# A forward list scheduler in place of a gap-filling one, for an eight-request decode kernel

## The chip, the cores and the metric

The kernel runs on one core of a Trainium2 chip. The core has a matrix engine (TensorE, PE), a vector engine (VectorE, DVE), a scalar engine (ScalarE, ACT) and a general one (GpSimd, POOL); a fifth queue (SyncE, SP) issues the DMA transfers. Each engine works off its own instruction stream strictly in the order in which the program was written for it, and waits on semaphores where it needs another engine's result. The metric is the device time of one execution in microseconds; lower is better.

## The reference

Eight requests (batch 8, one token each, width 448) pass through four layers: attention, MLP, and the same attention and MLP again, each behind a layer norm and with a residual. Both attentions use the same cache, of which only the last 1024 positions count.

```python
def _A_ref(x, k_cache, v_cache, wq, wo):         # Hq 16, Hkv 8, Dh 256, W 1024
    q = (x @ wq).reshape(B, Sq, Hq, Dh).transpose(0, 2, 1, 3)
    k = jnp.repeat(k_cache[:, :, Sk - W:, :], rep, axis=1)
    v = jnp.repeat(v_cache[:, :, Sk - W:, :], rep, axis=1)
    scores = jnp.einsum("bhqd,bhkd->bhqk", q, k) * (Dh ** -0.5)
    o = jnp.einsum("bhqk,bhkd->bhqd", _softmax(scores, axis=-1), v)
    return o.transpose(0, 2, 1, 3).reshape(B, Sq, Hq * Dh) @ wo
def _B_ref(x, w1, w2):                           # F 1792
    return jnp.einsum("bsf,fd->bsd", _silu(jnp.einsum("bsd,df->bsf", x, w1)), w2)

x = x + _A_ref(_layernorm(x), A_k_cache, A_v_cache, A_wq, A_wo)
x = x + _B_ref(_layernorm(x), B_w1, B_w2)
x = x + _A_ref(_layernorm(x), A_k_cache, A_v_cache, A_wq, A_wo)
x = x + _B_ref(_layernorm(x), B_w1, B_w2)
```

## The kernel before

**The work of one request.** The kernel goes through the requests b = 0 to 7. The keys and values of one request are 16 loads of 512 KB, into a ring of 29 buffers (`slots`). Below, number 0 behind a letter is the first attention, 1 the second.

1. `KT` (L879): DVE transposes the eight key buffers in place, two instructions per buffer, 16 per request.
2. `S0` (L600): 64 score matmuls of the first attention, in two halves `S0.0` and `S0.1` of four heads each. The query blocks `qbd` for them come from POOL (`qbd1`, L568), two instructions per request. Then the softmax: maximum (L606), three small DVE steps `mT`, `mg`, `mb` (L612 to L616), two exponentials on ACT (L620), a transposition on PE (`pT`, L625) and its copy (L629).
3. `PV0` (L657 in row form, L686 in column form), then `wo` (L728), a fold that adds the partial rows (L752, L497), and the new x (`xbt`, L699).
4. The chain of the MLP: statistics (L703, L705), mean and variance on DVE (L708 to L713), the power on POOL (L715), `w1` (L490), tanh (L768), `w2` (L773), a fold, the new x (`x2b`, L699), statistics again.
5. `wq` (L786): the queries of the second attention, two halves of 16 matmuls, each copied by ACT (`qrow`, L791), turned by PE (L794), and made into the blocks of `qbd` (L579, L583), with the factor `maskr` (L781).
6. `S1` (two halves again, L600), its softmax, and `PV1` (L657). The last two layers behind it are done for all eight requests together at the end (L809 to L847).

`keep` (L745) are matmuls with zeros into columns that nothing reads.

**What ties requests together.** All work of POOL stands in program order, since every POOL task writes the key `pool_serial`; so `qbd1` of request b+1 comes behind the second power of request b. `mT` is one tile for both attentions, so the softmax of `S0` of request b+1 comes behind that of `S1` of request b. `S1.0` frees four key slots, and into them go the last three value loads of request b+1; the second half of `S1` and `PV1` free the rest.

**What sets the order.** No order is written by hand. Every piece of work is a `Task` with an engine, a duration (`dur`) and the keys that it reads and writes; `Plan.add` derives the dependences from the keys. `Plan.schedule` (L78 to L165) then gives every task a rank (the longest way from it to the end, by the durations and the latencies `LAT`), takes the ready tasks by rank, and puts each into the first gap of its engine that is long enough and not before its inputs are ready. A task taken later can so land ahead of one taken earlier. Loads keep their program order; a DVE task that reads a load counts the load as landed 1.5 us later (`LOAD_MARGIN`). The times of this plan only sort the tasks: `Plan.emit` writes each engine's stream in the order of the planned starts, with the semaphore waits that this order needs.

Of the kernel before, what the change touches and what calls it, by code (L numbers as in the profile page):

```python
# [1 line left out]

# [8 lines left out]
ACTF = mybir.ActivationFunctionType  # L11
AX = mybir.AxisListType

SEM_LAT = {"pe": 0.05, "dve": 0.04, "act": 0.04, "pool": 0.06, "sp": 0.06}
LAT = {"pe": 0.15, "dve": 0.07, "act": 0.09, "pool": 0.05, "sp": 0.0}
LOAD_MARGIN = 1.5


class Task:
    __slots__ = ("eng", "fns", "dur", "prio", "name", "deps", "idx", "ready", "end", "sem", "val",  # L20
                 "vc", "n_bytes", "start", "users", "rank")

    def __init__(self, eng, fns, dur, prio, name, n_bytes=0):
        self.eng, self.fns, self.dur, self.prio, self.name = eng, fns, dur, prio, name
        self.n_bytes = n_bytes
        self.deps = {}
        self.users = 0
        self.end = None


class Plan:
# [43 lines left out]
        self.tasks.append(t)  # L75
        return t

    def schedule(self, dma_lat=2.1):  # L78


        tasks = self.tasks
        n_left = [len(t.deps) for t in tasks]
        succ = [[] for _ in tasks]
        for t in tasks:
            for i in t.deps:
                succ[i].append(t)
        sp_next = [t for t in tasks if t.eng == "sp"]
        nxt = {}
        for a, b in zip(sp_next, sp_next[1:]):
            nxt[a.idx] = b  # L90
        for t in reversed(sorted(tasks, key=lambda t: t.idx)):
            r = 0.0
            for u in succ[t.idx]:
                lat = (0.0 if t.eng == "pe" else 0.04) if t.eng == u.eng else LAT[t.eng] + 0.05
                r = max(r, u.rank + lat)
            if t.eng == "sp":
                own = t.dur
                t.rank = max(own + dma_lat + r, (own + nxt[t.idx].rank) if t.idx in nxt else 0.0)
            else:
                t.rank = t.dur + r  # L100
        gaps = {e: [[0.0, 1e9]] for e in ("pe", "dve", "act", "pool")}
        sp_pos, sp_free, dma_free = 0, 0.0, 0.0
        heap, seq = [], 0

        def push(t):
            heapq.heappush(heap, ((-t.rank if t.eng != "sp" else -1e9), t.idx, t))

        def ready_of(t):
            r = 0.0
            for o, raw in t.deps.values():  # L110
                if o.eng != t.eng or o.eng == "sp":
                    lat = LOAD_MARGIN if o.eng == "sp" and t.eng == "dve" else LAT[o.eng]
                    r = max(r, o.end + lat + SEM_LAT[t.eng])
                elif raw and t.eng in ("dve", "act"):
                    r = max(r, o.end + LAT[t.eng] + 0.04)
                else:
                    r = max(r, o.end)
            return r

        for t in tasks:  # L120
            if n_left[t.idx] == 0 and t.eng != "sp":
                push(t)
        if n_left[sp_next[0].idx] == 0:
            push(sp_next[0])
        done = 0
        while heap:
            _, _, t = heapq.heappop(heap)
            r = ready_of(t)
            if t.eng == "sp":
                t.start = max(r, sp_free)  # L130
                sp_free = t.start + 0.6
                s = max(t.start + 0.3, dma_free)
                dma_free = s + t.dur
                t.end = dma_free + dma_lat
                sp_pos += 1
                if sp_pos < len(sp_next) and n_left[sp_next[sp_pos].idx] == 0:
                    push(sp_next[sp_pos])
            else:
                g = gaps[t.eng]
                for k, (g0, g1) in enumerate(g):  # L140
                    s = max(g0, r)
                    if s + t.dur <= g1 + 1e-9:
                        break
                t.start, t.end = s, s + t.dur
                new = []
                if s - g0 > 0.02:
                    new.append([g0, s])
                if g1 - t.end > 0.02:
                    new.append([t.end, g1])
                g[k:k + 1] = new  # L150
            done += 1
            for u in succ[t.idx]:
                n_left[u.idx] -= 1
                if n_left[u.idx] == 0:
                    if u.eng != "sp":
                        push(u)
                    elif sp_pos < len(sp_next) and u is sp_next[sp_pos]:
                        push(u)
        assert done == len(tasks), "no task can run"
        self.order = {e: sorted((t for t in tasks if t.eng == e), key=lambda t: (t.start, t.end))  # L160
                      for e in ("pe", "dve", "act", "pool")}
        self.order["sp"] = sp_next
        self.span = max(t.end for t in tasks)
        self.busy = {e: sum(t.dur for t in self.order[e]) for e in self.order}
        return self.order  # L165

    def emit(self):
# [85 lines left out]
def bass_interleave_layers__sliding_block_cached__dense_activation_silu__decode_kernel(  # L253
    nc, A_x, A_k_cache, A_v_cache, A_wq, A_wo, B_x, B_w1, B_w2, out
):
    NB, Sq, D = A_x.shape
    _, HKV, SK, DH = A_k_cache.shape
    HD = A_wq.shape[1]
    H = HD // DH
    F = B_w1.shape[1]  # L260
    W = min(4096, max(256, SK // 4))
    S0 = SK - W
    P = 128
# [45 lines left out]
    vn = sb("vn", [P, 1], F32)  # L309
# [42 lines left out]
    def bk(i):  # L352
        return [("bank", i)]
# [4 lines left out]
    def dve(fn, reads, writes, dur, prio, name=""):  # L358
        add("dve", fn, reads=reads, writes=writes, dur=max(0.06, dur - LAT["dve"]), prio=prio, name=name)
# [68 lines left out]

    def load_wo():
        dma(lambda e: e.dma_start(wo_sb[:].rearrange("p (c n) -> p c n", n=D),  # L430
                                  A_wo.rearrange("(c p) n -> p c n", p=P)), ["wo"], HD * D * 2, "wo", rate=340e3)

    def load_w2():
        dma(lambda e: e.dma_start(w2_sb[:].rearrange("p (c n) -> p c n", n=D),
                                  B_w2.rearrange("(c p) n -> p c n", p=P)), ["w2"], F * D * 2, "w2", rate=340e3)

    WO_R = ["wo"]
    W2_R = ["w2"]
# [10 lines left out]
    def load_v(s, b, g):  # L449
        if g >= 4:  # L450
            dma(lambda e: e.dma_start(slots[s][:, :].rearrange("v (q n) -> v q n", q=4),
                                      A_v_cache[b, g, S0:SK, :].rearrange("(q v uh) d -> v q (uh d)", q=4, uh=2)),
                [("slot", s)], W * DH * 2, "slot%d" % s, rate=340e3)
# [3 lines left out]
        dma(lambda e: e.dma_start(slots[s][:, :].rearrange("v (j n) -> v j n", j=4),  # L457
                                  src.rearrange("j (v uh) d -> v j (uh d)", uh=2)),
            [("slot", s)], W * DH * 2, "slot%d" % s, rate=340e3)


    def wq_l(o, i):
# [146 lines left out]

    def softmax(b, layer, prio):  # L610
        sc, lb, ei = SC[layer], LB[layer], layer
        dve(lambda e: e.transpose(mT[ei][:], mseg[ei][:]), [("mseg", ei), ("mseg", ei, 0), ("mseg", ei, 1)], ["mT"], 0.21, prio)  # L612
        dve(lambda e: e.tensor_reduce(
            mg[ei][:], mT[ei][:, 0:8].rearrange("p (q r) -> p r q", r=2), AX.X, ALU.min),
            ["mT"], [("mg", ei)], 0.16, prio)
        dve(lambda e: e.transpose(mb[ei][:].rearrange("p (q r) -> p q r", r=2),  # L616
                                  mg[ei][:].unsqueeze(1).broadcast_to([P, 16, 2])),
            [("mg", ei)], [("mb", ei)], 0.19, prio)
        for k2 in range(2):
            act(lambda e, k2=k2: e.activation(  # L620
                e_sb[ei][:, k2, :, :].rearrange("p uh (jj ul) -> p uh jj ul", ul=4),
# [15 lines left out]
           [("pT", ei), "ones_b"], bk(lb), (64, 1), prio, "l")  # L637
        dve(lambda e: e.tensor_reduce(  # L638
            l_sb[ei][:], bank[lb][:, C_L:C_L + 64].rearrange("p (n q r) -> p n r q", q=4, r=2), AX.X, ALU.add),
            bk(lb), [("l", ei)], 0.23, prio)  # L640
        dve(lambda e: e.reciprocal(rl_sb[ei][:], l_sb[ei][:]), [("l", ei)], [("rl", ei)], 0.25, prio)

    def pv_rows(b, layer, k2, prio, oT_dst, oT_key):

# [303 lines left out]
```

## Time and profile before

| | |
|---|---|
| three runs | 306.78, 306.21, 304.15 us (median 306.21) |
| profiled execution | span 306.6 us from the first to the last instruction; no other time is listed for it |
| PE busy | 216.4 us, 71% of the span |
| DVE busy | 155.9 us, 51% |
| ACT, POOL busy | 50.6 us (17%), 22.6 us (7%) |
| moved by DMA | 78.29 MB, mean 255 GB/s |
| granted TensorE clock, mean | 0.844 |

The spans of the page are those of one execution. Its chain of waits is the work that ended last, followed back from the end: each piece of it starts when the piece before has released it. A mean busy share says little here, since the kernel has three stretches with different limits: a start in which the weights and the first request's cache are loaded, a middle in which one request follows the other, and an end with the last two layers.

### The profile page before, as it was taken

To read this page: it belongs to the slowest core of one execution; us is meant where nothing else is said; L and a number is where in the kernel's file an instruction comes from. 1 tells how busy PE (TensorE), PEld (TensorE's weight loads), DVE (VectorE), ACT (ScalarE), POOL (GpSimd) and SP (SyncE) were. 2 spreads that over 40 slices of the span, in tenths; PEclk is the share of its full clock that TensorE was granted. 3 is DMA by queue.
4 is the path that set the end of the run, shared out by engine and by line. 5 is a ranking of instruction groups with operands and counts; after the bars stand their busy time and mean duration, and the time that the engine had idled before them with its cause. 6 is when DMAs were issued, how large, how long until landed. Compare 5 with 4: busy or idle time off the path is not lost.

```text
span 306.6 us, 9727 instructions
## 1 busy us (share of the span) xinstructions
PE 216.4 (71%) x4406; PEld 122.5 (40%) x4406; DVE 155.9 (51%) x480; ACT 50.6 (17%) x119; POOL 22.6 (7%) x41
## 2 busy tenths in 40 slices
PE   1143367856987788697879778778878697897662
PEld 0231125333543355254525453355345524543340
DVE  6278101288276737754765446635774568213122
ACT  1000100201311131104110402031114021312111
POOL 1110000010002000200020000200020002000010
PEclk9999999967977879769956975797599959979695
DMA  7999999999993899179936993399729983300000
GB/s 262 352 407 379 362 356 351 407 373 353 406 367 100 293 407 359 44 226 387 375 117 215 383 379 128 91 396 387 228 61 350 406 286 89 124 2 2 0 2 1
DMA packets 50152, 78.29 MB, mean 255 GB/s; under 512 B 2224, under 2 KB 41024, under 8 KB 49728
## 3 DMA queue, kind: packets, MB, share of 16 engines
q1 hardware_dynamic: 50112, 77.68, 71.9%
q8 instruction: 34, 0.56, 0.8%
q14 instruction: 6, 0.05, 0.0%
HBM read 77.67 MB, written 0.01 MB: 253 GB/s over the span
## 4 chain that ended last, share of the span: by engine, by line
PE 53%; DVE 16%; SPq 13%; issue 6%; ACT 5%; DMA 3%; POOL 2%; DVEq 0%; ACTq 0%
PE bank L600 8%; PE bank L657 8%; SPq L457 8%; PE bank L786 7%; PE bank L686 4%; PE bank L773 4%; PE bank L728 4%; PE bank L490 3%; PE bank L745 3%; DMA w_sb<-in_B_w_dram 3%; DVE slot L879 3%; DVE qbd L583 2%; PE bank L625 2%; ACT e_sb L620 2%; DVE mseg L606 2%
## 5 line engine op out<-in xcount | busy, mean ns | idle before, releaser
L879 DVE STREAM_TRANSPOSE slot<-slot 128x512 uint32<-128x512 uint32 x128 | 82.9, 686 | 6.0 <-DMA slot<-in_A_k_cache_dram 6.0
L600 PE MATMUL bank<-slot,qbd 128*8 128x256 bf16 x1024 | 44.0, 320 | 21.8 <-DVE mseg L606 9.4
L600 PEld LDWEIGHTS bank<-slot,qbd 128*8 128x8 bf16 x1024 | 24.8, 95 | 34.6 <-DVE mseg L606 11.6
L657 PE MATMUL bank<-slot,pT_sb 128*2 128x256 bf16 x768 | 29.5, 299 | 6.8 <-DMA slot<-in_A_v_cache_dram 3.9
L715 POOL TENSOR_TENSOR rhalf<-var,nhalf 128x1 f32<-128x1 f32 x16 | 8.7, 544 | 238.7 <-DVE var L713 238.7
L745 PE MATMUL bank<-sel,cols_b 128*128 128x480 bf16 x56 | 23.1, 494 | 2.6 <-DVE vpos L764 2.6
L786 PE MATMUL bank<-wq_sb,x2b 128*1 128x512 bf16 x256 | 23.1, 496 | 2.2 <-DVE x2b L699 2.2
L657 PEld LDWEIGHTS bank<-slot,pT_sb 128*2 128x2 bf16 x768 | 16.7, 87 | 14.7 <-DMA slot<-in_A_v_cache_dram 5.5
L620 ACT ACTIVATE e_sb<-bank,mb 128x256 bf16<-128x256 f32 x32 | 13.4, 471 | 53.9 <-DVE mb L616 53.7
L638 DVE TENSOR_REDUCE l_sb<-bank 128x16 f32<-128x64 f32 x16 | 3.6, 225 | 34.0 <-PE bank L633 26.6
L686 PEld LDWEIGHTS bank<-pT_sb,slot 128*128 128x128 bf16 x512 | 15.0, 97 | 10.5 <-issue 9.9
L490 PE MATMUL bank<-xbt,w_sb 128*128 128x32 bf16 (+1 forms) x504 | 16.2, 181 | 3.8 <-DVE xbt L699 2.0
L606 DVE TENSOR_REDUCE mseg<-bank 128x1 f32<-128x256 f32 x32 | 12.9, 410 | 11.7 <-PE bank L600 11.7
L686 PE MATMUL bank<-pT_sb,slot 128*128 128x2 bf16 x512 | 16.9, 164 | 2.6 <-issue 1.4
L728 PE MATMUL bank<-wo_sb,oT 128*1 128x448 bf16 x224 | 15.6, 387 | 3.8 <-DVE oT L670 1.8
L791 ACT ACTIVATE qrow<-bank 128x512 bf16<-128x512 f32 x16 | 9.6, 597 | 49.0 <-PE bank L786 46.9
L490 PEld LDWEIGHTS bank<-xbt,w_sb 128*128 128x128 bf16 x504 | 14.5, 100 | 4.7 <-DVE xbt L699 2.5
L692 DVE TENSOR_TENSOR oT<-bank,rl_sb 128x4 bf16<-128x4 f32 x32 | 5.1, 161 | 18.9 <-PE bank L686 18.9
L625 PE MATMUL bank<-ident,e_sb 128*128 128x128 bf16 x64 | 7.2, 243 | 9.9 <-ACT e_sb L620 9.9
L773 PE MATMUL bank<-w_sb,hT 128*1 128x448 bf16 x112 | 12.9, 555 | 1.4 <-DVE hT L770 0.9
L664 ACT ACTIVATE e_sb<-bank 128x256 bf16<-128x256 f32 x24 | 8.4, 382 | 25.4 <-PE bank L657 25.4
L568 POOL TENSOR_TENSOR qbd<-q1s,mask 128x256 bf16<-128x256 bf16 x16 | 9.8, 613 | 13.5 <-DVE q1s L556 12.4
(122 smaller groups left out, 193.3 us busy)
## 6 DMA issues: line engine op xcount, KB each, us to landing
slot<-in_A_k_cache_dram SPq DMA_DIRECT2D x64, 512.0 KB, 8.7
slot<-in_A_v_cache_dram SPq DMA_DIRECT2D x64, 512.0 KB, 9.2
wo_sb<-in_A_wo_dram SPq DMA_DIRECT2D x1, 3584.0 KB, 26.2
wq_sb<-in_A_wq_dram SPq DMA_DIRECT2D x3, 1024.0 KB, 6.9
w_sb<-in_B_w_dram SPq DMA_DIRECT2D x1, 1568.0 KB, 13.0
w_sb<-in_B_w_dram SPq DMA_DIRECT2D x1, 1344.0 KB, 11.4
wq_sb<-in_A_wq_dram SPq DMA_DIRECT2D x2, 256.0 KB, 10.2
w_sb<-in_B_w_dram SPq DMA_DIRECT2D x2, 112.0 KB, 10.0
```

Source lines behind the costliest of these rows:

```text
L457: dma(lambda e: e.dma_start(slots[s][:, :].rearrange("v (j n) -> v j n", j=4), src.rearrange("j (v uh) d -> v j (uh d)", uh=2)), [("slot", ...
L490: fns.append(lambda e, o=o, i=i, r=r: e.matmul(bank[bank_i][:, col + (o - outs[0]) * n:col + (o - outs[0] + 1) * n], lhs(o, i), r.broadcas ...
L600: fns.append(lambda e, cb=cb, par=par, j=j, kvh=kvh, kv=kv: e.matmul(bank[sc][32 * j:32 * j + 8, k2 * 256:(k2 + 1) * 256], qbd[qi][:, kvh, ...
L606: dve(lambda e: e.tensor_reduce(mseg[layer][:, k2:k2 + 1], bank[sc][:, k2 * 256:(k2 + 1) * 256], AX.X, ALU.max, negate=True), bk(sc), [("m ...
L620: act(lambda e, k2=k2: e.activation(e_sb[ei][:, k2, :, :].rearrange("p uh (jj ul) -> p uh jj ul", ul=4), bank[sc][:, k2 * 256:(k2 + 1) * 2 ...
L657: fns.append(lambda e, q=q, uh=uh, j=j, vv=vv: e.matmul(bank[ob][32 * j:32 * j + 2, c0:c0 + DH], pT_sb[ei][:, k2 * 2 + uh, j * 8 + 2 * q:j ...
L686: fns.append(lambda e, a=a, q=q, uh=uh: e.matmul(bank[vb][:, c0 + 2 * a:c0 + 2 * a + 2], vs[:, (2 * q + uh) * DH + a * P:(2 * q + uh) * DH ...
L728: fns.append(lambda e, i=i, c=c, kvh=kvh: e.matmul(bank[XB][32 * c:32 * c + 1, 0:D], oT1[:, i % 2, i // 2:i // 2 + 1], wo_sb[:, i * D:(i + ...
L745: pe([lambda e: e.matmul(bank[YB][:, 32:512], zero_b.broadcast_to([P, P]), sel[:].rearrange("p c m -> p (c m)")[:, 0:480], start=False, st ...
L773: pe([lambda e, f=f: e.matmul(bank[XB][32 * (f % 4):32 * (f % 4) + 1, 0:D], hT[:, f:f + 1], w2_sb[:, f * D:(f + 1) * D], start=(f < 4), st ...
L786: pe([lambda e, j=j, c=c, k2=k2, wb=wb: e.matmul(bank[wb][32 * j:32 * j + 1, :], x2[:, xcol(c, k2):xcol(c, k2) + 1], wq_sb[:, c * HD + ((4 ...
L879: dve(lambda e, v=v: e.transpose(v, v), [("slot", s)], [("slot", s)], 0.67, prio, "KT")
```

## The change

The body of `Plan.schedule` is new. It walks forward in time: at each step it takes the engine whose next start is earliest, and on it the most urgent of the tasks that could start there now. If a more urgent one will be able to start within 0.664 (`HOLD`) of the chosen task's duration, it takes that one instead and leaves the engine idle until then, unless a task fits in between. Urgency is the rank plus an offset per kind of task (`BIAS`, in us). A kind is the engine, the name without the request, and a letter: `a` for the first attention, `b` for the chain up to `S1`, `c` for the second softmax and `PV1`, `e` for start and end. Durations of single kinds are replaced (`OCC`), those of PE multiplied by 1.032, the latencies between engines are a table (`TAIL`, `HOP`), and the loads have other rates and latencies. `LOAD_MARGIN` is gone. Some DVE tasks get names, so that `OCC` and `BIAS` can find them. The tasks, their instructions, their dependences, the buffers, the order of the loads and `Plan.emit` are as before.

```diff
-SEM_LAT = {"pe": 0.05, "dve": 0.04, "act": 0.04, "pool": 0.06, "sp": 0.06}
 LAT = {"pe": 0.15, "dve": 0.07, "act": 0.09, "pool": 0.05, "sp": 0.0}
-LOAD_MARGIN = 1.5
+TAIL = {"pe": 0.17, "dve": 0.07, "act": 0.09, "pool": 0.02, "sp": 0.0}
+HOP = {"pe": {"pe": 0.0, "dve": 0.05, "act": 0.05, "pool": 0.06, "sp": 0.05},
...
+OCC = {"dve:KT": 0.635, "dve:max": 0.35, "dve:maskr": 0.16, "dve:nmean": 0.10, "dve:vn": 0.15, "dve:var4": 0.15,
+       "dve:vpos": 0.17, "dve:hT": 0.12, "dve:xb": 0.10, "dve:oTev": 0.10, "dve:qT2": 0.16, "dve:qbd": 0.36,
+       "act:exp": 0.38, "act:oev": 0.30, "act:pTev": 0.20, "act:qrow": 0.51, "act:rowb": 0.50, "act:tanh": 0.22,
+       "pool:pow": 0.53, "pool:pow8": 1.63, "pool:qbd1": 0.60}
+SP_ISSUE, DMA_FIRST, DMA_LAST = 0.47, 1.2, 2.2
+HOLD, PE_SCALE = 0.664, 1.032
+BIAS = {"dve.KT.a": 22.4, "pe.S0.0.a": -78.2, "dve.max.a": 23.1, "pe.PV0.0.0.a": -52.9, "dve.oTev.a": 42.5,
+        "pe.PV0.1.0.a": -21.9, "pe.PV0.1.1.a": 34.2, "dve.xb.b": 61.8, "dve.nmean.b": 76.2, "dve.vn.b": 130.7,
+        "dve.var4.b": 69.1, "pe.w1.b": -131.8, "dve.vpos.b": 70.6, "dve.hT.b": 26.1, "dve.maskr.b": 46.5,
+        "dve.qT2.b": 102.1, "dve.qbd.b": 99.0, "pe.S1.0.b": -54.5, "dve.max.b": 66.3, "dve.mT.c": 39.4,
+        "pe.l.c": 48.6, "pe.PV1.0.0.c": 53.0, "pe.PV1.0.1.c": 55.7, "pe.PV1.0.2.c": 50.5, "pe.PV1.0.3.c": 51.6,
+        "pe.oT.c": -34.2, "pe.PV1.1.1.c": 94.7, "pe.PV1.1.2.c": -48.5}
...
-    def schedule(self, dma_lat=2.1):
+    def schedule(self):
...
-                g = gaps[t.eng]
-                for k, (g0, g1) in enumerate(g):
-                    s = max(g0, r)
-                    if s + t.dur <= g1 + 1e-9:
-                        break
-                t.start, t.end = s, s + t.dur
...
+        urgency = [t.rank + BIAS.get(t.kind, 0.0) for t in tasks]
...
+        def at(t):
+            return max(ready[t.idx], free[t.eng])
+
+        def best(of):
+            return max(of, key=lambda t: (urgency[t.idx], -t.idx))
+
+        while n_done < len(tasks):
+            if n_load < len(loads) and not left[loads[n_load].idx]:
+                t = loads[n_load]
+                n_load += 1
+                t.start = at(t)
+                free["sp"] = t.start + SP_ISSUE
+                bus = max(t.start + DMA_FIRST, bus) + occ[t.idx]
+                t.end = bus + DMA_LAST
             else:
...
+                now, e = min((min(at(t) for t in waiting[e]), i, e)
+                             for i, e in enumerate(waiting) if waiting[e])[::2]
+                can = waiting[e]
+                t = best([u for u in can if at(u) <= now + 1e-9])
+                sooner = [u for u in can if urgency[u.idx] > urgency[t.idx] and at(u) < now + HOLD * occ[t.idx]]
+                if sooner:
+                    t = best(sooner)
+                    between = [u for u in can if at(u) + occ[u.idx] <= at(t) + 1e-9]
+                    if between:
+                        t = best(between)
+                can.remove(t)
+                t.start = at(t)
+                free[e] = t.start + occ[t.idx]
+                t.end = free[e]
...
-    def dma(fn, writes, n_bytes, key, reads=(), rate=400e3):
+    def dma(fn, writes, n_bytes, key, reads=(), rate=411.2e3):
...
-            [("slot", s)], W * DH * 2, "slot%d" % s, rate=340e3)
+            [("slot", s)], W * DH * 2, "slot%d" % s, rate=349.5e3)
```

More of the change, by code (lines that the diff above doesn't have):

```diff
@@ L1 @@
-import heapq
 import numpy as np
@@ L28, in __init__ @@
         self.end = None
+        part = "e" if prio < 0 or prio >= 9000 else "abc"[(prio % 100 >= 60) + (prio % 100 >= 70)]
+        self.kind = ".".join([eng, *(p for i, p in enumerate(name.split(".")) if i != 1), part])
 class Plan:
@@ L76, in add @@
         return t
-    def schedule(self, dma_lat=2.1):
+    def schedule(self):
         tasks = self.tasks
-        n_left = [len(t.deps) for t in tasks]
         succ = [[] for _ in tasks]
         for t in tasks:
[L85 to L95, printed above, removed]
-            if t.eng == "sp":
-                own = t.dur
-                t.rank = max(own + dma_lat + r, (own + nxt[t.idx].rank) if t.idx in nxt else 0.0)
-            else:
[L100 to L138, printed above, removed]
-                g = gaps[t.eng]
-                for k, (g0, g1) in enumerate(g):
-                    s = max(g0, r)
-                    if s + t.dur <= g1 + 1e-9:
-                        break
-                t.start, t.end = s, s + t.dur
[L145 to L160, printed above, removed]
@@ new lines, in schedule, with lag @@
+            for o, raw in t.deps.values():
+                succ[o.idx].append((t, raw))
+        loads = [t for t in tasks if t.eng == "sp"]
+        following = {a.idx: b for a, b in zip(loads, loads[1:])}
+        occ = [OCC.get(t.eng + ":" + t.name, t.dur) * (PE_SCALE if t.eng == "pe" else 1.0) for t in tasks]
+        def lag(t, u, raw):
+            if t.eng != u.eng or t.eng == "sp":
+                return TAIL[t.eng] + HOP[t.eng][u.eng]
+            return TAIL[t.eng] + HOP[t.eng][t.eng] if raw and t.eng != "pe" else 0.0
@@ new lines, in schedule @@
+        for t in reversed(tasks):
+            r = max([u.rank + lag(t, u, raw) for u, raw in succ[t.idx]], default=0.0)
+            t.rank = occ[t.idx] + r
+            if t.eng == "sp":
+                t.rank += DMA_FIRST + DMA_LAST
+                if t.idx in following:
+                    t.rank = max(t.rank, occ[t.idx] + following[t.idx].rank)
+        urgency = [t.rank + BIAS.get(t.kind, 0.0) for t in tasks]
+        left = [len(t.deps) for t in tasks]
+        ready = [0.0] * len(tasks)
@@ new lines, in schedule @@
+        free = {e: 0.0 for e in ("pe", "dve", "act", "pool", "sp")}
+        waiting = {e: [t for t in tasks if t.eng == e and not left[t.idx]] for e in ("pe", "dve", "act", "pool")}
+        n_load, bus, n_done = 0, 0.0, 0
+        def at(t):
[10 more added lines that the diff above has]
+                t.end = bus + DMA_LAST
+            else:
+                now, e = min((min(at(t) for t in waiting[e]), i, e)
[12 more added lines that the diff above has]
+                t.end = free[e]
+            n_done += 1
+            for u, raw in succ[t.idx]:
+                ready[u.idx] = max(ready[u.idx], t.end + lag(t, u, raw))
+                left[u.idx] -= 1
+                if not left[u.idx] and u.eng != "sp":
+                    waiting[u.eng].append(u)
@@ L161, in schedule @@
+        self.order = {e: sorted((t for t in tasks if t.eng == e), key=lambda t: (t.start, t.idx))
                       for e in ("pe", "dve", "act", "pool")}
-        self.order["sp"] = sp_next
-        self.span = max(t.end for t in tasks)
-        self.busy = {e: sum(t.dur for t in self.order[e]) for e in self.order}
+        self.order["sp"] = loads
         return self.order
@@ L458, in load_v @@
                                   src.rearrange("j (v uh) d -> v j (uh d)", uh=2)),
-            [("slot", s)], W * DH * 2, "slot%d" % s, rate=340e3)
+            [("slot", s)], W * DH * 2, "slot%d" % s, rate=349.5e3)
     def wq_l(o, i):
```

20 lines of the change are left out of this document (12 added, 8 removed).

## The prediction

> **What bounds the kernel now.** I read the page first, for the shares of the span.
>
> ```profile
> span 306.6 us, 9727 instructions
> PE 216.4 (71%) x4406; PEld 122.5 (40%) x4406; DVE 155.9 (51%) x480; ACT 50.6 (17%) x119; POOL 22.6 (7%) x41
> GB/s 262 352 407 379 362 356 351 407 373 353 406 367 100 293 407 359 44 226 387 375 117 215 383 379 128 91 396 387 228 61 350 406 286 89 124 2 2 0 2 1
> PE 53%; DVE 16%; SPq 13%; issue 6%; ACT 5%; DMA 3%; POOL 2%; DVEq 0%; ACTq 0%
> ```
>
> No engine is full, and TensorE carries only 53% of the chain that ended last. The GB/s row (40 slices of 7.7 us) is near 400 for the first twelve slices and then falls once per request, to 100, 44, 117, 91, 61. So loads bound the start, and in the middle the loads wait for buffers that the requests free. The middle is a loop of dependent steps. Second I looked at the chain of waits in order of time (start, length, engine and line), for the pace of that loop. These are its pieces at `wq` (L786) and at the first exponential behind `S1` (L620), for requests 1 to 7, with what lies between for requests 3 and 5:
>
> ```profile
> 93.37 1.63 PE bank L786 x15
> 106.55 0.85 ACT e_sb L620 x2
> 125.84 1.03 PE bank L786 x16
> 138.44 0.85 ACT e_sb L620 x2
> 155.83 1.88 PE bank L786 x16
> 160.64 1.88 PE bank L600 x30
> 162.52 1.71 PE bank L786 x16
> 164.22 1.28 PE bank L600 x22
> 166.97 1.09 PE bank L600 x32
> 169.29 0.85 ACT e_sb L620 x2
> 189.72 1.25 PE bank L786 x15
> 201.69 0.85 ACT e_sb L620 x2
> 221.31 1.03 PE bank L786 x16
> 223.72 0.96 PE bank L786 x16
> 225.65 0.87 PE bank L600 x21
> 230.69 0.85 ACT e_sb L620 x2
> 250.19 1.72 PE bank L786 x16
> 259.99 0.85 ACT e_sb L620 x2
> 277.04 1.03 PE bank L786 x16
> 285.68 0.85 ACT e_sb L620 x2
> ```
>
> From the start of `wq` to the start of that exponential, requests 1 to 7 take 13.18, 12.60, 13.46, 11.97, 9.38, 9.80 and 8.64 us (differences of the starts). From there to the next `wq` it is 19.29, 17.39, 20.43, 19.62, 19.50 and 17.05. The first stretch has the larger spread, and the reason stands in the rows. Request 3 does the first half of `wq` at 155.83, then `S1.0` at 160.64, then the second half of `wq` at 162.52, then `S0` of request 4, and only at 166.97 `S1.1`. Request 5 does the second half of `wq` at 223.72, before `S1.0`. The stretch of request 3 from `wq` to `S1.0` is 4.81 us, and TensorE needs 1.88 of it for the first half. The timeline (start, length, engine, line) shows what ties `S0` down, and what the last request does with that time:
>
> ```profile
> 158.80 0.54 POOL L715 TENSOR_TENSOR rhalf<-var,nhalf 128x1 f32<-128x1 f32 x1 [6.75 <-DVE var L713]
> 159.42 1.31 POOL L568 TENSOR_TENSOR qbd<-q1s,mask 128x256 bf16<-128x256 bf16 x2
> 162.91 1.29 DVE L879 STREAM_TRANSPOSE slot<-slot 128x512 uint32<-128x512 uint32 x2
> 278.51 1.03 PE L786 MATMUL bank<-wq_sb,x2b 128*1 128x512 bf16 x16
> ```
>
> `S0` of request 4 cannot start before the second power and the `qbd1` behind it (160.7), whatever the order, and its last two transposes end at 164.2. The second half of `wq` depends on neither; request 7 has it 1.47 us behind the first.
>
> **The change, part by part.** Nothing is added or removed: all instructions, waits between tasks and loads stay, and only the order on PE, DVE, ACT and POOL moves. So the sum is over what is moved.
>
> *The second half of `wq`.* In the new urgency `wq` has no offset, `S1.0` has -54.5 and `S0.0` has -78.2; a request takes about 31 us, so these offsets put `S1.0` and `S0.0` about two requests back. The second half of `wq` is ready together with the first, and the walk forward in time takes the most urgent task that can start. I conclude that it comes directly behind the first half, or behind the statistics, in every request, as in 5 to 7, and that `S0` fills what stays free. Then the stretch is that of request 5, 9.4 us with transposes and `S0` in it. Against 13.18, 12.60, 13.46, 11.97, 9.38, 9.80 that is 3.8 + 3.2 + 4.1 + 2.6 + 0 + 0.4 = 14.1 us. Its ends: the 8.64 us of request 7, which has no `S0` and no transposes beside it, would give 4.5 more (18.6). If only half of the requests follow, it is 7.
>
> What is late next: the transposes for `S0`, and the value loads that wait for `S1.0`.
>
> ```profile
> L879 DVE STREAM_TRANSPOSE slot<-slot 128x512 uint32<-128x512 uint32 x128 | 82.9, 686 | 6.0 <-DMA slot<-in_A_k_cache_dram 6.0
> 77.00:261.65 184.65, 147.49 (x3036) 83.28 (x3036) 108.19 (x314) 35.11 (x85) 13.87 (x24) 0.81 0.76 270
> 256.64 2.13 SPq L451 DMA_DIRECT2D slot<-in_A_v_cache_dram  x3
> 266.85 0.95 PE L686 MATMUL bank<-pT_sb,slot 128*128 128x2 bf16 x32
> ```
>
> The group's row gives 16 x 0.686 = 11.0 us of transposes per request. The window over six requests (columns: length, then busy PE, PEld, DVE, ACT, POOL, clock, DMA share, GB/s) has DVE busy for 108.19 of 184.65 us, 18.0 of 30.8 per request. At 27.8 us per request DVE would be busy for 65%, so the transposes fit, if their order lets them. Request 6 frees its value buffers at 256.64, 3.35 us ahead of its exponential, and the matmuls that read them at 266.85 show no wait (no bracket). With the shorter order already in place there, the value loads are hidden.
>
> *The rest of the loop.* The statistics of the MLP come ahead of `w1` (offset -131.8), the second half of `PV1` is split (+94.7, then -48.5), and the small DVE steps of the chain (+26 to +131) go ahead of transposes (+22.4). The loop is one chain here, so it gains only where a step stands behind foreign work. Its ends: all requests like the best loaded one (17.39) would be 1.9 + 0 + 3.0 + 2.2 + 2.1 = 9.2 us less. Against that, holding can idle DVE by 0.664 x 0.635 = 0.42 us before a transpose (both figures the diff's); one such hold that helps nobody per request is 2.5 us more over six. I take 0.5 us less per request, 3 in all, nearer to the unchanged rows, since four of the five loaded ones lie at 19.3 to 20.4 and show no single foreign piece.
>
> *The start.*
>
> ```profile
> 68.17 3.18 PE L600 MATMUL bank<-slot,qbd 128*8 128x256 bf16 x64 [0.94 <-DVE slot L879]
> 68.68 4.84 DVE L879 STREAM_TRANSPOSE slot<-slot 128x512 uint32<-128x512 uint32 x8
> 73.44 0.71 DVE L606 TENSOR_REDUCE mseg<-bank 128x1 f32<-128x256 f32 x2
> ```
>
> The score matmuls end at 71.35, and their maxima wait until 73.44 behind eight transposes. With +66.3 on the maximum of `S1` against +22.4 it goes first, which is worth up to 2.1 us. The same transposes gate `S0` of request 1, so I take 1, from 0 to 2.1. Before that the load order decides, and it stays. Behind 277.04 there is one request and nothing to reorder: 0, give or take 1.
>
> Sum: 14.1 + 3 + 1 = 18.1 us, from a span of 306.6 to 288.5. The median of the runs is 306.21, 0.4 below the span, so 288 for the runs.
>
> **The clock.** It falls to half in every request. Three stretches of request 3 (columns as above; the clock is third from the right):
>
> ```profile
> 150.90:152.40 1.50, 1.01 (x20) 0.45 (x16) 1.25 (x5) 0.26 (x1) 0.54 (x1) 1.00 1.10 348
> 152.40:154.00 1.60, 1.22 (x14) 0.37 (x14) 1.44 (x4) 0.05 (x1) 0.00 (x0) 0.58 1.10 348
> 164.70:166.30 1.60, 1.60 (x33) 0.65 (x25) 0.23 (x1) 0.17 (x1) 0.00 (x0) 0.50 1.08 383
> ```
>
> At half clock the 16 matmuls of `wq` take 1.88 us instead of 1.03, and the 32 of `S1` 1.88 instead of 1.09. I leave these spells as they are in the sum. [...]
>
> **The rivals.**
> *Nothing gained (304 to 308).* The order comes out different, but the loop closes elsewhere: `S1.1` is early, and `S0` of the next request, tied to the POOL order and to 11 us of transposes, makes its softmax late instead. For it speaks that the transposes of request 4 end at 164.2, 1.3 us later than `S1.1` would start in the new order (the exponential at 155.83 + 9.4, less the 2.32 us that request 3 has from `S1.1` to it: 162.9). Against it speak requests 5 and 6, which do both in 9.4 and 9.8 us. Time: 306.
>
> *Faster still (272 to 280).* The gaps behind `wq` close, and the clock stays whole for longer. Two half-rate pieces per request, 0.85 and 0.79 us, come off the chain: 1.64 x 6 = 9.8 us below 288, or 278. For it: request 5 has `wq` at 1.03. Against it: the clock falls before `wq`, in a part of the chain whose work stays.
>
> *Slower (about 316).* Each engine works in order, so a transpose whose load has not landed blocks DVE, and the chain's small steps behind it. In the rows DVE waits for a load once, 6.0 us at the start, and never again. `LOAD_MARGIN` (1.5 us) is gone, and transposes have +22.4. Eight buffers per request at 0.5 us of wait, an estimate of about 0.4 of the 1.3 us that a buffer of 512 KB takes at the 400 GB/s of the page's row, would be 4.0 us, on requests 1 to 7 some 28 us: 288 + 28 = 316. It decides from 2.6 us per request on (18.1 / 7). Against it: the new loads are timed too, and the chain's steps carry larger offsets than the transposes. The start shows the mechanism (eight transposes, 2.1 us).
>
> **How the numbers follow.** The forecast (its ends are 306.2 - 18.6 - 9.2 - 2.1 = 276 and 306.2 - 7 + 2.5 = 302; its own range is 280 to 297, since the ends of three terms seldom come together) gets 0.55, faster still 0.15, nothing gained 0.13, slower 0.17. About 1% can be told from no change in this kernel. Faster by over 1% is 0.55 + 0.15 = 0.70, within 1% 0.13, slower 0.17. The range from 272 to 308 leaves out the slower case and little of the faster.
>
> **What would show it.** Right: in the chain of waits the two halves of `wq` stand next to each other in all requests, ahead of `S1.0`; from `wq` to the exponential it is 9 to 10 us in requests 1 to 6; the page's GB/s row falls less deep between requests. Wrong: idle time of L879 put down to key loads in the middle, a softmax of `S0` that waits for transposes, or a stretch from the exponential to the next `wq` of more than 20 us, which would mean that the scheduler moved the foreign work there. If the clock is over 0.9 in the middle, the gain is larger, and for another reason than I give.

## The result

The changed kernel takes 283.3 us (median of 4 runs, 282.9 to 285.2) against 305.2 us of the kernel before on the same chip (302.6 to 306.8). The ratio is 0.930, with a 95% interval from 0.923 to 0.937. Medians are over all runs of a kernel, and ratios over its faster runs alone (within 1.5% of its fastest) against those of the kernel before on the same chip. The prediction was 288 us, 272 to 308. The profiled execution has a span of 281.5 us, against 306.6 before. The page of the changed kernel (its lines are two lower than before, so L600 is L598 here, and L786 is L784):

```profile
span 281.5 us, 9739 instructions
PE 203.1 (72%) x4406; PEld 119.2 (42%) x4406; DVE 155.1 (55%) x480; ACT 51.4 (18%) x119; POOL 22.6 (8%) x41
GB/s 250 357 409 384 372 349 359 376 407 354 361 407 364 130 356 410 357 142 393 401 329 189 398 384 246 225 409 375 192 237 407 377 182 220 8 2 2 2 0 1
PE 58%; SPq 14%; DVE 13%; issue 5%; ACT 4%; DMA 3%; POOL 1%; ACTq 0%; DVEq 0%
```

TensorE does the same 4406 matmuls in 203 us of busy time instead of 216; that it needs less for the same work is the clock (in the middle 0.89 instead of 0.81, see below). The GB/s row falls less deep between requests: 130, 142 and 189 instead of 100, 44 and 117. The stretch from `wq` to the first exponential behind `S1`, for request 3, in the timeline of the changed kernel:

```profile
144.32 1.03 PE L784 MATMUL bank<-wq_sb,x2b 128*1 128x512 bf16 x16 [0.28 <-DVE x2b L697]
145.79 1.03 PE L784 MATMUL bank<-wq_sb,x2b 128*1 128x512 bf16 x16
147.82 0.63 PE L598 MATMUL bank<-slot,qbd 128*8 128x256 bf16 x16
148.57 0.63 PE L598 MATMUL bank<-slot,qbd 128*8 128x256 bf16 x16
149.32 3.31 PE L598 MATMUL bank<-slot,qbd 128*8 128x256 bf16 x96
152.83 0.84 ACT L618 ACTIVATE e_sb<-bank,mb 128x256 bf16<-128x256 f32 x2 [5.18 <-DVE mb L614]
```

The second half of `wq` follows the first after 1.47 us, all score matmuls come behind it, and the clock is 1.00 over the whole stretch (144.32 to 152.83). The stretch is 8.51 us; before, it was 13.46.

The loop of requests 1 to 6, cut at the starts of the same instructions in both traces (`wq`, first exponential of `S1`, first matmul of `PV1`, the new x of the first attention, `w2`, next `wq`), summed over the six:

| from, to | before | after | difference | predicted |
|---|---|---|---|---|
| `wq` to exponential | 70.4 us | 51.6 us | -18.8 | -14.1 |
| exponential to `PV1` | 10.0 | 10.5 | +0.5 | |
| `PV1` to new x | 60.5 | 57.2 | -3.3 | |
| new x to `w2` | 24.6 | 23.3 | -1.3 | |
| `w2` to next `wq` | 18.2 | 17.5 | -0.8 | |
| the last four together | 113.3 | 108.5 | -4.8 | -3 |
| start to `wq` of request 1 | 93.4 | 91.6 | -1.8 | -1 |
| `wq` of request 7 to the end | 29.6 | 29.9 | +0.3 | 0 |

The differences add up to 25.1 us, which is what the spans differ by.

### The profile page after: what moved, and what is told of

The parts are those of the page before. It is cut to its first block, busy times and chain, and to the rows that moved or that the text cites. A ratio compares the mean times of both kernels' runs of the same rounds, so it can differ in the third digit from the quotient of the medians.

```text
span 281.5 us, 9739 instructions
## 1 busy us (share of the span) xinstructions
PE 203.1 (72%) x4406; PEld 119.2 (42%) x4406; DVE 155.1 (55%) x480; ACT 51.4 (18%) x119; POOL 22.6 (8%) x41
## 4 chain that ended last, share of the span: by engine, by line
PE 58%; SPq 14%; DVE 13%; issue 5%; ACT 4%; DMA 3%; POOL 1%; ACTq 0%; DVEq 0%
PE bank L655 9%; SPq L455 9%; PE bank L598 8%; PE bank L784 6%; PE bank L488 6%; PE bank L743 5%; PE bank L684 5%; PE bank L726 4%; PE bank L771 4%; DMA w_sb<-in_B_w_dram 3%; DVE mseg L604 3%; DVE slot L877 3%; SPq L449 2%; SPq L443 2%; PE bank L735 1%
## 5 line engine op out<-in xcount | busy, mean ns | idle before, releaser
L877 DVE STREAM_TRANSPOSE slot<-slot 128x512 uint32<-128x512 uint32 x128 | 84.9, 691 | 9.9 <-DMA slot<-in_A_k_cache_dram 9.4
L598 PE MATMUL bank<-slot,qbd 128*8 128x256 bf16 x1024 | 40.3, 299 | 7.3 <-DVE mg L611 4.1
L655 PE MATMUL bank<-slot,pT_sb 128*2 128x256 bf16 x768 | 28.3, 291 | 4.3 <-ACT pT_sb L627 3.4
L598 PEld LDWEIGHTS bank<-slot,qbd 128*8 128x8 bf16 x1024 | 22.9, 89 | 17.8 <-DVE mseg L604 5.2
L618 ACT ACTIVATE e_sb<-bank,mb 128x256 bf16<-128x256 f32 x32 | 14.1, 471 | 55.1 <-DVE mb L614 55.1
L743 PE MATMUL bank<-sel,cols_b 128*128 128x480 bf16 x56 | 21.4, 461 | 2.6 <-DVE vpos L762 2.6
L604 DVE TENSOR_REDUCE mseg<-bank 128x1 f32<-128x256 f32 x32 | 13.5, 423 | 10.1 <-PE bank L598 9.0
L488 PE MATMUL bank<-xbt,w_sb 128*128 128x32 bf16 (+1 forms) x504 | 15.2, 180 | 5.0 <-issue 4.6
L784 PE MATMUL bank<-wq_sb,x2b 128*1 128x512 bf16 x256 | 16.9, 384 | 2.2 <-DVE x2b L697 2.2
L488 PEld LDWEIGHTS bank<-xbt,w_sb 128*128 128x128 bf16 x504 | 14.0, 99 | 5.5 <-issue 5.1
L662 ACT ACTIVATE e_sb<-bank 128x256 bf16<-128x256 f32 x24 | 9.2, 383 | 22.2 <-PE bank L655 22.2
L771 PE MATMUL bank<-w_sb,hT 128*1 128x448 bf16 x112 | 11.4, 502 | 0.0
```

Of the source, the lines that this page charges most:

```text
L488: fns.append(lambda e, o=o, i=i, r=r: e.matmul(bank[bank_i][:, col + (o - outs[0]) * n:col + (o - outs[0] + 1) * n], lhs(o, i), r.broadcas ...
L598: fns.append(lambda e, cb=cb, par=par, j=j, kvh=kvh, kv=kv: e.matmul(bank[sc][32 * j:32 * j + 8, k2 * 256:(k2 + 1) * 256], qbd[qi][:, kvh, ...
L604: dve(lambda e: e.tensor_reduce(mseg[layer][:, k2:k2 + 1], bank[sc][:, k2 * 256:(k2 + 1) * 256], AX.X, ALU.max, negate=True), bk(sc), [("m ...
L618: act(lambda e, k2=k2: e.activation(e_sb[ei][:, k2, :, :].rearrange("p uh (jj ul) -> p uh jj ul", ul=4), bank[sc][:, k2 * 256:(k2 + 1) * 2 ...
L655: fns.append(lambda e, q=q, uh=uh, j=j, vv=vv: e.matmul(bank[ob][32 * j:32 * j + 2, c0:c0 + DH], pT_sb[ei][:, k2 * 2 + uh, j * 8 + 2 * q:j ...
L743: pe([lambda e: e.matmul(bank[YB][:, 32:512], zero_b.broadcast_to([P, P]), sel[:].rearrange("p c m -> p (c m)")[:, 0:480], start=False, st ...
```

## The experiments

In the first three, one stretch of TensorE's order of the changed kernel is put back at the boundaries after requests 1 to 6, once the scheduler is done (`reorder` puts the tasks of the stretch into the listed order, `B` being the request); every other order is that of the changed kernel.

**Both the second half of `wq` and `S0.0` back behind `S1.0`.**

```diff
+        self.reorder([("wq", 1), ("stat", 1), ("keep", 1), ("qturn", 1), ("qsel", 1), ("S1.B.0", 4), ("wq", 1), ("S0.B+1.0", 3), ("qturn", 1),
+                      ("S0.B+1.0", 1), ("xinit", 1), ("qsel", 1), ("S1.B.1", 4), ("S0.B+1.1", 4)], range(1, 7))
...
```

> The changed kernel, with one stretch of TensorE's order put back to that of the kernel before for the boundaries after requests 1 to 6: S1.0 first, then the second half of wq, then S0.0 of the next request, then S1.1. All else is as changed. Theory (the second half of wq ahead of S1.0, and S0.0 in the gap, are the gain): from wq to the exponential the requests 1 to 6 go back from 8.5 us to 11.5 to 13 us, 18 to 25 us in all, so 300 to 306 us. Rival (the clock made about half of it, and the order of DVE another part): with the clock whole in that stretch it goes back to 10.5 to 11 us only, 293 to 298 us.

Measured: 305.1 us, ratio 0.980 (0.972 to 0.987). Its ten runs spread from 297.8 to 309.0 us and the profiled one is the slowest, so I take no rows from it. The ratio answers to about 300 us, but it rests on three of the ten runs (297.8 to 302.0). Most of the gain of 0.930 goes back with this stretch alone: by the ratio at the lower edge of what the theory gave, by the median at its upper end, and either way above the rival.

**Only the second half of `wq` back.**

```diff
+        self.reorder([("wq", 1), ("stat", 1), ("keep", 1), ("qturn", 1), ("qsel", 1), ("S0.B+1.0", 2), ("S1.B.0", 4), ("wq", 1),
+                      ("S0.B+1.0", 2), ("qturn", 1), ("xinit", 1), ("qsel", 1), ("S1.B.1", 4), ("S0.B+1.1", 4)], range(1, 7))
...
```

> The changed kernel, with only the second half of wq (and the two small steps that need it) put behind S1.0 at the boundaries after requests 1 to 6; S0.0 stays where the change puts it. Theory: 1.03 us of matmuls, 0.60 of copy and 0.26 of turning now stand between S1.0 and S1.1, about 1.9 us per request, 10 to 13 us in all, so 293 to 297 us, nearly all of what putting back both gives. Rival (it is S0.0 that counts): below 286 us.

Measured: 305.8 us, ratio 0.995 (0.991 to 0.999). That is about twice the loss that I expected (293 to 297 us): nearly the whole gain hangs on this one step. By the ratios it even loses more than putting both back did, which no theory had and these runs do not explain; by the medians the two are alike. From `wq` to the exponential the requests 1 to 6 take 10.8 to 13.1 us, 12.2 on average, instead of 8.6. For request 3, first in the timeline, then in two windows (length, busy PE, PEld, DVE, ACT, POOL, clock, DMA share, GB/s):

```profile
156.36 2.73 PE L616 MATMUL bank<-slot,qbd 128*8 128x256 bf16 x48 [0.32 <-POOL qbd L584]
158.88 1.42 PE L802 MATMUL bank<-wq_sb,x2b 128*1 128x512 bf16 x16
165.82 0.84 ACT L636 ACTIVATE e_sb<-bank,mb 128x256 bf16<-128x256 f32 x2 [4.86 <-DVE mb L632]
```

```profile
152.97:156.37 3.40, 2.06 (x35) 0.93 (x36) 3.07 (x8) 0.60 (x1) 1.16 (x2) 0.98 0.02 6
156.37:158.97 2.60, 2.60 (x52) 1.69 (x56) 1.04 (x2) 0.00 (x0) 0.61 (x1) 0.50 0.03 6
```

With `wq` gone from the gap, TensorE has 2.06 us of work in 3.40, and then the clock is 0.50 while it does the score matmuls: 48 of them take 2.73 us. So the step seems to have two effects, a longer chain and a slower clock; the fifth experiment separates them.

**Only `S0.0` back.**

```diff
+        self.reorder([("wq", 1), ("stat", 1), ("keep", 1), ("wq", 1), ("qturn", 1), ("qsel", 1), ("xinit", 1), ("qturn", 1), ("S1.B.0", 2),
+                      ("qsel", 1), ("S1.B.0", 2), ("S0.B+1.0", 4), ("S1.B.1", 4), ("S0.B+1.1", 4)], range(1, 7))
...
```

> The changed kernel, with only S0.0 of the next request put behind S1.0 at the boundaries after requests 1 to 6; the second half of wq stays where the change puts it. Theory: the first 16 of its 32 matmuls (0.56 us) move from a gap into the way of S1.1, so at most 0.6 us per request, 283 to 287 us. Rival (it is S0.0 that counts): 290 us or more.

Measured: 287.2 us, ratio 0.935 (0.929 to 0.941), at the upper edge of the theory, and not told apart from 0.930. The place of `S0.0` is worth at most some 4 us (the difference of the medians; by the ratios it is about 1.5).

**The kernel before, with only the second half of `wq` moved up.**

```diff
...
+        for b in range(5):
+            wq = [i for i, t in enumerate(o) if t.name == "wq"]
+            keep = next(i for i in range(wq[2 * b], len(o)) if o[i].name == "keep")
...
+            o.insert(keep + 1, o.pop(wq[2 * b + 1]))
```

> The kernel before, with only the second half of wq put directly behind the statistics in requests 0 to 4, nothing else. Theory: 1.7 us (at half clock) comes off the way to S1.1, but two transposes stand between the maximum of S1.0 and the step of DVE that makes the second query block, which leaves about 1.4 us: 5 x 1.4 = 7 us, so 296 to 300 us. Rival (the place of wq alone does nothing without the new order of DVE): within 2 us of the kernel before.

Measured: 299.5 us, ratio 0.971 (0.962 to 0.981), as expected. So this one move, in the old order of everything else, gives two fifths of the gain. The exponential of requests 1 to 4 comes 10.0 to 12.6 us behind `wq` instead of 12.0 to 13.5.

**Idle work in the place of `wq`.** The second experiment, with five more matmuls of zeros in the gap:

```diff
             o[first:last + 1] = new
+            k = next(t for t in new if t.name == "keep")
+            k.fns = k.fns * 6
```

> As the second experiment (the second half of wq behind S1.0), with five more matmuls of zeros in the gap that it leaves, so that TensorE has about as much to do there as in the changed kernel. The second experiment lost 3.7 us per request, of which 1.9 us is the longer chain. Theory (the rest is the clock: the idle gap lets it fall to half just ahead of S1): the clock stays whole through S1, from wq to the exponential it is 10.4 to 10.8 us instead of 12.2, and the time is 292 to 297 us. Rival (the rest is waiting that has nothing to do with the clock): no gain from idle work, 302 to 308 us.

Measured: 294.6 us, ratio 0.949 (0.940 to 0.959), inside the theory's range. Work that computes nothing wins back about half of what putting `wq` back had lost by the medians, and 70% by the ratios. The same two windows as above, for request 3 (the profiled execution took 295.6 us):

```profile
150.55:153.95 3.40, 2.91 (x42) 1.42 (x43) 3.03 (x8) 0.60 (x1) 1.15 (x2) 1.00 0.00 0
153.95:156.55 2.60, 2.60 (x76) 1.90 (x80) 1.04 (x2) 0.05 (x1) 0.61 (x1) 1.00 0.02 6
```

With 2.91 us of work in the gap's 3.40 the clock stays at 1.00 behind it. From `wq` to the exponential it is 10.8 to 11.2 us, 11.0 on average. So of the 3.6 us per request between 12.2 and 8.6, about 1.2 is the clock in this stretch and 2.4 the longer chain, for which I had 1.9. Over the whole span (304.2, 293.8 and 281.5 us for `wq` back, `wq` back with idle work, and the changed kernel) it is 10.4 us for the idle work and 12.3 for the order; the ratios (0.995, 0.949, 0.930) would split it 14 to 6. That both count is shown, the share only roughly.

**Which part of the scheduler does it.** Three kernels: the new one with an empty table of offsets; the forward walk (with holding and the new table of latencies) with no offsets and with the old durations and load rates; and the old gap-filling walk with the new durations and rates.

```diff
-BIAS = {"dve.KT.a": 22.4, "pe.S0.0.a": -78.2, ...
+BIAS = {}
```

> The changed kernel with an empty table of offsets (BIAS); forward walk, holding, and task times as changed. The place of the second half of wq is the same in this order. Theory (the place of wq is the main gain, and it comes from the forward walk, not from the offsets that my prediction named): 284 to 290 us. Rival (the offsets carry the gain): 295 us or more.

Measured: 287.7 us, ratio 0.935 (0.929 to 0.941).

```diff
+BIAS = {}
-        occ = [OCC.get(t.eng + ":" + t.name, t.dur) * (PE_SCALE if t.eng == "pe" else 1.0) for t in tasks]
+        occ = [t.dur for t in tasks]
...
-    def dma(fn, writes, n_bytes, key, reads=(), rate=411.2e3):
+    def dma(fn, writes, n_bytes, key, reads=(), rate=400e3):
...
```

> The forward walk with holding, without offsets, and with the task durations and load rates of the kernel before. Theory: the second half of wq stands ahead of S1.0 in all requests in this order too, so 285 to 293 us. Rival (the measured durations carry the gain): 298 us or more.

Measured: 289.1 us, ratio 0.942 (0.938 to 0.946).

```diff
     def schedule(self, dma_lat=2.1):                      # the body of before
         tasks = self.tasks
+        for t in tasks:
+            t.dur = OCC.get(t.eng + ":" + t.name, t.dur) * (PE_SCALE if t.eng == "pe" else 1.0)
...
```

> The gap-filling scheduler of before with the new task durations and load rates. In its order the second half of wq still stands inside or behind S1.0 in requests 1 and 2 and ahead of it in requests 4 and 5. Theory (it is the walk and the place of wq): 295 to 305 us, between the two. Rival (the measured durations carry the gain): 283 to 290 us.

Measured: 304.7 us, ratio 0.991 (0.983 to 0.999).

The theory holds in all three. The forward walk gives 5.8 of the 7.0 per cent. Durations and offsets add 0.7 and 0.5, each within what the intervals leave open, and better durations alone do next to nothing for the old walk. In both orders without offsets the second half of `wq` stands directly behind the `keep` that follows the first, in every request: 1.5 to 2.5 us behind the first half, as the starts in the trace show.

**The orders of the other engines alone.**

```diff
+    forward = dict(pl.schedule())
...
+    pl.schedule_gap()                                     # the scheduler and the times of before
+    for e in ('dve', 'act', 'pool'):
+        pl.order[e] = forward[e]
```

> TensorE's order of the kernel before; the orders of DVE, ACT and POOL of the changed kernel. (The reverse is not possible: the new TensorE order and the old order of DVE wait for each other.) Theory (the gain is TensorE's order at S1): 299 to 307 us. Rival (the order of DVE, chain steps ahead of transposes, carries a good part): 295 us or less.

Measured: 315.9 us, ratio 1.036 (1.022 to 1.050): slower than either theory gave. In the middle it is as the theory says: requests 1 to 4 take 13.20, 12.96, 13.01 and 12.98 us from `wq` to the exponential, as before (13.18, 12.60, 13.46, 11.97). The loss lies at the start, where request 0 takes 20.2 us instead of 15.8. The timeline of this kernel there:

```profile
72.80 0.21 DVE L703 STREAM_TRANSPOSE mT<-mseg 128x32 f32<-128x32 f32 x1
72.94 2.45 DVE L970 STREAM_TRANSPOSE slot<-slot 128x512 uint32<-128x512 uint32 x4
75.31 0.39 DVE L697 TENSOR_REDUCE mseg<-bank 128x1 f32<-128x256 f32 x1
75.62 2.47 DVE L970 STREAM_TRANSPOSE slot<-slot 128x512 uint32<-128x512 uint32 x4
78.02 0.12 DVE L704 TENSOR_REDUCE mg<-mT 128x2 f32<-128x8 f32 x1
```

Between two steps of the same softmax, `mT` and `mg`, stand eight transposes of the next request, 4.9 us. The new order of DVE puts them there for a TensorE that is further on by then; each engine's order only fits the orders of the others. It is also a case of my rival for slower, a chain behind transposes, though none of these transposes shows a wait for its load. The reverse (only TensorE's order new) can't be built, since the two orders wait for each other, so it wasn't tried.

**More and less idle work.** Two more matmuls of zeros behind `wo` in requests 1 to 6; and the changed kernel without any of its 56:

```diff
+        for t in self.order["pe"]:
+            if t.kind == "pe.keep.a" and 100 < t.prio < 700:
+                t.fns = t.fns * 2
```

> The changed kernel with two more matmuls of zeros behind wo in requests 1 to 6, ahead of the stretch in which the clock still falls. They cost at most 0.4 us per request. Theory (the clock falls where TensorE had little to do just before): the clock stays whole through w2 in some requests, which is worth about 1.2 us in each of them, so 278 to 284 us. Rival (the idle work comes too early or is too little): 283 to 287 us.

```diff
-                    for fn in t.fns:
+                    for fn in t.fns if t.name != "keep" or t.users else ():
```

> The changed kernel without any of the 56 matmuls of zeros; the order of all else as changed. Theory of the clock: the half-rate spells grow and cost more than the matmuls of zeros did, 286 to 298 us. Rival (they are dead weight in the new order, which keeps TensorE busy by itself): 276 to 282 us.

The first has 282.0 us, ratio 0.925 (0.915 to 0.934), the fastest median of all, but its interval overlaps that of the changed kernel. It cannot be called better. The second has 301.3 us, ratio 0.980 (0.970 to 0.989), by its median above the 298 us that the theory gave at most: without the idle work, five of the seven per cent are gone. The middle (first matmul of `PV1` of request 0 to that of request 6) of the changed kernel, of the one with more and of the one without:

```profile
75.40:237.80 162.40, 136.15 (x3036) 79.97 (x3036) 106.31 (x314) 36.12 (x86) 13.84 (x24) 0.89 0.87 311
```

```profile
74.63:235.96 161.33, 137.74 (x3049) 80.76 (x3049) 106.41 (x314) 36.15 (x86) 13.84 (x24) 0.91 0.89 316
```

```profile
76.96:255.63 178.67, 144.51 (x2995) 82.08 (x2995) 107.46 (x314) 36.16 (x86) 13.84 (x24) 0.73 0.79 280
```

The clock (third from the right) is 0.89, 0.91 and 0.73; in the middle of the kernel before it was 0.81. The matmuls of zeros are not dead weight in the new order. They are what its clock rests on.

**Idle work in the old order.** The kernel before with nothing moved, and five more matmuls of zeros in the gap ahead of `S1.0` of requests 0 to 4:

```diff
+            if t.name == "keep" and len(t.fns) == 1 and t.prio < 500:
+                t.fns = t.fns * 6
```

> The kernel before, its order untouched, with five more matmuls of zeros in the idle gap ahead of S1.0 in requests 0 to 4. Theory (half of what the old order lost there was the clock): S1.0, the second half of wq and S0.0 run at full rate in requests 1 to 4, about 2 us in each, so 296 to 301 us. Rival (the clock there is decided elsewhere): 304 to 308 us.

Measured: 295.5 us, ratio 0.974 (0.960 to 0.987), just under the 296 to 301 us of the theory. Request 3 of this kernel:

```profile
154.45 1.11 PE L603 MATMUL bank<-slot,qbd 128*8 128x256 bf16 x32 [0.72 <-DVE qbd L586]
155.35 1.07 PE L789 MATMUL bank<-wq_sb,x2b 128*1 128x512 bf16 x16
160.88 0.84 ACT L623 ACTIVATE e_sb<-bank,mb 128x256 bf16<-128x256 f32 x2 [3.82 <-DVE mb L619]
```

```profile
153.90:156.50 2.60, 2.05 (x60) 1.62 (x64) 2.53 (x5) 0.04 (x1) 0.61 (x1) 1.00 0.02 6
```

The old order is untouched, `wq` still stands behind `S1.0`, and the same pieces that took 1.88 and 1.71 us take 1.11 and 1.07. The stretch (`wq` at 150.50) is 10.4 us instead of 13.5. Five matmuls that compute nothing give the old order as much as moving `wq` did.

## Why the prediction was right, and where it was not

*Bound and place: right.* The loop of dependent steps set the pace, and the first stretch held the gain: 18.8 of 25.1 us.

*The second half of `wq`: right as the step, mis-sized.* I had 14.1 us, with 18.6 as the end; it was 18.8. The term took request 5's 9.4 us as what every request would reach, and 8.64, from a request with nothing beside it, as the end. All six reached 8.5 to 8.8 with `S0` and transposes beside them. The last 0.8 us against request 5 answer to the second half itself: there it came 2.3 us behind the start of the first, now 1.5.

*Why it moves: half right.* I named two reasons, the offsets of `S1.0` and `S0.0`, and the walk that takes the most urgent task that can start. The offsets are not needed: without any it stands in the same place, and the ratio is 0.935 where the full change has 0.930. The walk is the reason, as the plan that the kernel before computes shows for request 3. There the second half of `wq` has 0.92 us and a lower rank than `S1.0` (103.2 against 104.5), so `S1.0` and the small steps ahead of it are placed first. They leave gaps of 0.68, 0.44 and 0.67 us behind `keep`, and none is long enough. In request 5 it ranks ahead of `S1.0` and is placed before it. Moving forward in time, TensorE takes whatever is ready when it would be idle, while the gap-filling walk, even with the new durations, still placed it inside `S1.0` in requests 0 to 3.

*The clock: the step that failed.* I left the half-rate spells "as they are in the sum". They changed: 0.81 to 0.89 in the middle, just short of the 0.9 that I had named as the sign of another reason. Filling the gap did not only take `wq` off the chain, it also kept the clock up behind it (1.00 behind 2.91 us of work in 3.40, in the fifth experiment, and 0.50 behind 2.06, in the second). Idle work alone wins back 10 to 14 us of what putting `wq` back loses, and moves the old kernel by 2.6%. Request 5, my yardstick, already ran this stretch at a clock of 1.00 (221.31 to 230.69 of the kernel before; request 3 had 0.61 over its 13.46 us), so the estimate contained the effect without my naming it; that the number came near is partly luck. My case "faster still" took it that the clock stays whole for longer once the gaps close. That was my assumption, and no run had shown it then; the fifth and the last experiment did. It also had the pieces: in the changed kernel the first half of `wq` takes 1.03 us in five of the six requests, and the score matmuls of request 3 run at 1.10 us per 32. But these pieces were in request 5's 9.4 us already and could not come off 288 a second time. The slow spell ahead of `wq` is still there: in the last 1.5 us before it the clock is 0.50 to 0.88 in requests 2 to 6.

*The rest of the loop and the start: near.* -4.8 for -3, with 0.5 us lost between the exponential and `PV1` that I had not listed; -1.8 for -1; +0.3 for 0 at the end.

*The slower case did not come.*

```profile
L877 DVE STREAM_TRANSPOSE slot<-slot 128x512 uint32<-128x512 uint32 x128 | 84.9, 691 | 9.9 <-DMA slot<-in_A_k_cache_dram 9.4
```

DVE's waits for loads are 9.4 us instead of 6.0. One of 6.5 lies at the start, so the other five hold 2.9 us together, where 28 would have been needed. *Nothing gained* did not come either: the maxima of `S0` follow those of `S1` within 1.1 us in the new order, so that the transposes were in time.

## What to carry to other kernels

Where one chain sets the pace, look at what stands ready in the queue beside each idle gap; a scheduler that walks forward in time fills these gaps by itself, and here that was worth more than better durations or tuned offsets. Work taken out of a gap on TensorE cost twice here: in the second experiment the chain was about 2.4 us longer per request, and the clock of 0.50 on the work behind the gap took about 1.2 us more. So ask what the clock was in the rows that an estimate is taken from. And try the cheapest test first: idle matmuls in the gap, with the order untouched, tell in one run how much of a gap's price is the clock (here a ratio of 0.974).

## What the runs showed of the hardware

**The clock fell although TensorE had been busy for most of the time just before.** With TensorE busy for 2.06 us of 3.40 the clock was at 0.50 afterwards (request 3 of the second experiment), with 2.91 of 3.40 at 1.00 (request 3 of the fifth).

**The busy time alone did not decide it.** Here are two stretches of the kernel with the second half of `wq` put back, with the ones behind them, for requests 3 and 5:

```profile
152.97:156.37 3.40, 2.06 (x35) 0.93 (x36) 3.07 (x8) 0.60 (x1) 1.16 (x2) 0.98 0.02 6
156.37:158.97 2.60, 2.60 (x52) 1.69 (x56) 1.04 (x2) 0.00 (x0) 0.61 (x1) 0.50 0.03 6
216.11:219.51 3.40, 2.06 (x36) 0.94 (x36) 3.08 (x8) 0.60 (x1) 1.16 (x2) 1.00 0.01 3
219.51:222.11 2.60, 2.60 (x76) 1.91 (x80) 1.04 (x2) 0.04 (x1) 0.61 (x1) 1.00 0.03 6
```

TensorE is busy for 2.06 us in both, and the clock is 0.50 behind the first and 1.00 behind the second, where 52 and 76 matmuls stand in 2.60 us. What decides it, no run shows.

**Matmuls of zeros count.** Both the five in the old order's gap (0.974) and the 56 of the changed kernel (0.980 without, 0.930 with) show it. So does the clock. In the old order, in the 2.60 us from 3.40 us behind the start of `wq` of request 3, it is 1.00 with the five and was 0.50 without (159.23 to 161.83 of the kernel before). In the middle of the changed kernel it is 0.89 with the 56 and 0.73 without.

**TensorE stops about once per request.** The chain of waits of the changed kernel has stops ("issue", time in which the engine waited for nothing that the profile shows) in requests 4 and 6 and none in request 7 at the place where request 4 has it (`w1`, L488). No load runs there any more (4 GB/s from 242 to 250, against 399 and 405 around the stops of requests 4 and 6):

```profile
164.34 1.16 issue
214.25 1.59 issue
246.99 1.43 PE bank L488 x56
```

The stop of 1.0 to 1.6 us falls among the many short matmuls of the column form of `PV0` and of `w1` (164 and 180 ns each on average in the changed kernel), in each of requests 1 to 6 and in neither of the kernels at request 7; the kernel before has such stops too (0.4 to 1.5 us, not in request 3). What TensorE waits for there is not shown. In the changed kernel the six stops are 7.3 us of the chain; no run was made to remove them.
